# Rebuilding the low bits of three weight tiles on ScalarE instead of shifting on VectorE, in a retention and SwiGLU kernel

## The chip, the cores and the metric

The kernel runs on one core of a Trainium2 chip. The metric is the device time of one execution, in microseconds (us). Before the change it is 654.19 us, the median of three runs (653.77 to 654.31). Engines are called by the names of the profile: PE is TensorE's matmul, PEld its weight load, DVE is VectorE, ACT is ScalarE, POOL is GpSimd, SP is SyncE. SP issues most DMA transfers and computes nothing.

## What is computed

The reference is a retention layer (a linear attention with a decay for each head) whose output goes through an RMS norm and a SwiGLU block. Cut to what matters here:

```python
# attention: 4 x 8 heads x 768 x 64, blocks of 64, decay lam per head
out[:, :, sl] = intra + inter            # (q k^T * decay) v  +  (q * decay) state
x   = out as rows of tokens              # 3072 tokens x 512
rms = sqrt(mean(x * x, axis=-1) + 1e-06)
xn  = x / rms * rms_g
g   = xn @ w_gate                        # 512 x 1536
val = xn @ w_val                         # 512 x 1536
y   = (g * sigmoid(g) * val) @ w_out     # 1536 x 512
```

The three weight matrices arrive as float64, so each weight is 8 bytes in device memory. The kernel loads them as pairs of 32-bit words and builds a float32 from each pair itself, by shifts and an OR on the integer words. That conversion is what the change touches.

## The kernel before

**Tiles.** The 1536 hidden columns are 12 tiles `f` of 128, and the 3072 tokens are 6 groups `m` of 512. A unit `(m, f)` makes gate and val of one tile for one group, the SiLU and the product, and adds into the output. PE works with split operands: each weight and each activation is a high and a low half in fp16, and three products (high by high, low by high, high by low) stand for one.

**Start of the kernel.** Until about 37 us the kernel loads the first group's q, k and v, runs its retention on PE, forms the norm, and converts the first weight tiles. PE's first projection (`pg`, line 761) needs the normed activations `xn` (DVE, line 714), cast to a high half by ACT (`x`, line 719) and to a low half by DVE (line 722), and the split weights `wg`, `wv` of tile 0. From there on PE runs units of projection and output product (lines 780 to 782), with the retention of group 1 in between.

**The conversion of a tile** takes these steps, for gate and val together (128 x 1024 words) or, for tile 1, in two halves of 128 x 512:

- `lift` (line 218, ACT): reads the high word of each pair as a float, with a scale and a slope for negative numbers that put sign and exponent where the shift wants them, and writes `bits`.
- `convert` part 0 (line 227, DVE): `bits << 3`, in place.
- `convert` part 1 (line 230, DVE): `(low word >> 29) | bits`, which puts in the low three bits of the mantissa.
- `square` (line 440, ACT; rows named `junk`, followed by a read of the accumulator), then `norm` (line 445, PE; `pn`), `scale` (lines 452 and 456, DVE; `e` and `sc`), then `high` (line 463, ACT) and `low` (line 467, DVE), which split the tile into `wg` and `wv`.

The output weights of a tile (`raw_o`) go through `lift_o` and `convert_o`, which use the same two functions on 128 x 512, then a split into `wo` by ACT (line 246) and DVE (line 250).

**Buffers.** The raw pairs of tile 0 land in the tile `partial`, those of the later tiles in the four buffers `in` (named `raw_gv`), those of the output weights in the two buffers `raw_o`. The next load into a buffer is issued by SP, in order, once the step that reads it last is done (lines 87, 99 and 105 are the loads of q, k and v, of gate and val, and of the output weights). The PSUM bank `pg` holds the gate product of a unit, then the state sums `pst` (line 540) of the retention, so these wait for the SiLU `sg` (line 1022, ACT) that reads the gate product. The SBUF tiles of `sg` rotate with the squares `sq` (line 606), which POOL adds up (line 612).

**The order.** Each engine runs its instructions in the order in which they are written. A planner in the kernel (`Plan`) sets it before anything is built: each step has an engine, a cost and a due time, written out by hand in calls of `step(...)`, and a table of shifts moves single due times. The conversion of a tile is planned by `convert_steps` (`halved_steps` for tile 1), with ACT for the lift, 0.7 us of DVE for part 0 and 1.23 us for part 1.

Of the kernel before, what the change touches and what calls it, by code (L numbers as in the profile page):

```python
# [9 lines left out]
F32 = mybir.dt.float32  # L10
# [3 lines left out]
AF = mybir.ActivationFunctionType  # L14
ALU = mybir.AluOpType
PSUM = bass.MemoryType.PSUM

P = 128
G = 512
# [4 lines left out]
def retention_swiglu_kernel(  # L24
# [19 lines left out]
    nc = tc.nc  # L44
# [10 lines left out]
    const = ctx.enter_context(tc.tile_pool(name="const", bufs=1))  # L55
# [158 lines left out]
    def lift(bits, raw):  # L214

        nc.scalar.activation(
            bits.bitcast(F32), raw[:, :, 1].bitcast(F32), AF.Prelu, scale=2.0**-112,
            alpha=2.0**32,  # L220
        )

    def convert(bits, raw, part=None):


        if part != 1:
            nc.vector.tensor_single_scalar(bits, bits, 3, op=ALU.logical_shift_left)
        if part == 0:
            return
        nc.vector.scalar_tensor_tensor(  # L230
            bits, raw[:, :, 0], 29, bits, ALU.logical_shift_right, ALU.bitwise_or
        )
# [159 lines left out]
    class Weights:  # L392
# [22 lines left out]
        def lift(self, i=None):  # L415
            if not i:
                self.start()
            if i is None:
                lift(self.w, self.raw)
            else:  # L420
                lift(self.wi[i], self.raw[:, i * G : (i + 1) * G])

        def convert(self, i=None, part=None):
            if i is None:
                convert(self.w, self.raw, part)
            else:
                convert(self.wi[i], self.raw[:, i * G : (i + 1) * G], part)

        def lift_o(self):
            self.raw_o = raws.pop((self.f, "o"))  # L430
            lift(self.bits, self.raw_o)

        def convert_o(self, part=None):
            convert(self.bits, self.raw_o, part)
# [1452 lines left out]
```

## Time and profile before

| | |
|---|---|
| median of three runs | 654.19 us (653.77 to 654.31) |
| the profiled execution | 654.11 us, span 652.3 us |
| granted TensorE clock | 0.999 |
| busy, share of the span | PE 98%, DVE 67%, ACT 51%, POOL 23% |
| 27 to 37 us, of 10.00 | PE 8.46, DVE 9.52, ACT 9.08, POOL 3.48 |
| 40.5 to 47 us, of 6.50 | PE 6.44, DVE 6.20, ACT 5.19, POOL 1.28 |

The span runs from the first to the last instruction, and the execution's own time has 1.8 us more around it. In a row of the timeline the first number is the start in us from the span's start, the second the duration in us, then engine, line, operation, output `<-` input, shape and count; in brackets stands how long the engine sat idle before it and what ended the wait. Instructions of one engine overlap a little in such rows: the next one starts some 0.1 us before the last has ended.

### The profile page before, as it was taken

How to read it: one execution, taken by the hardware profiler on the slowest of the kernel's cores; microseconds unless marked ns; L12 is line 12 of the kernel's file. 1: busy time of each engine (PE TensorE's matmuls, PEld its weight loads, DVE VectorE, ACT ScalarE, POOL GpSimd, SP SyncE). 2: the span in 40 equal slices, each digit the busy share in tenths (PEclk: the TensorE clock that was granted, in tenths of full speed). 3: DMA queues.
4: the chain of work that ended last, by engine and by line, in shares of the span. 5: the costliest groups of instructions: out<-in, count | busy, mean ns of one | idle time of the engine just before them, and what ended most of it. 6: DMA issues, size and time to landing. Idle time of an engine off the chain costs nothing.

```text
span 652.3 us, 12342 instructions
## 1 busy us (share of the span) xinstructions
PE 642.5 (98%) x5016; PEld 442.0 (68%) x5016; DVE 433.9 (67%) x836; ACT 334.8 (51%) x676; POOL 149.4 (23%) x133
## 2 busy tenths in 40 slices
PE   7999999999999999999999999999999999999997
PEld 6846564755656645777777777777777777777774
DVE  6798897968997659656589634587543488544334
ACT  2876876756774444444545533335444334533332
POOL 2213040003477654354703011002010101100000
PEclk9999999999999999999999999999999999999999
DMA  8956653411002400101300311100220000000001
GB/s 328 327 211 221 238 191 133 169 58 65 1 24 91 146 2 1 65 4 63 130 2 2 130 65 65 66 1 1 97 99 1 2 2 1 33 33 1 2 1 65
DMA packets 14314, 51.13 MB, mean 78 GB/s; under 512 B 1713, under 2 KB 1969, under 8 KB 12849
## 3 DMA queue, kind: packets, MB, share of 16 engines
q1 hardware_dynamic: 13968, 50.21, 21.5%
q8 instruction: 39, 0.64, 0.4%
q10 hardware_dynamic: 288, 0.14, 0.1%
q14 instruction: 19, 0.15, 0.1%
HBM read 44.05 MB, written 6.29 MB: 77 GB/s over the span
## 4 chain that ended last, share of the span: by engine, by line
PE 95%; DVE 3%; DMA 1%; issue 0%; POOL 0%; ACT 0%; DVEq 0%; ACTq 0%
PE pa L948 20%; PE pb L948 15%; PE acc L780 10%; PE acc L782 10%; PE acc L781 10%; PE pg L761 9%; PE pv L761 9%; PE pa L507 4%; PE po L572 3%; PE po L583 3%; PE pst L540 2%; PE pss L628 1%; DMA cs<-in_consts_dram 1%; DVE xn L714 0%; DVE pw L159 0%
## 5 line engine op out<-in xcount | busy, mean ns | idle before, releaser
L996 ACT COPY tx<-pa 128x256 f32<-128x256 f32 x144 | 53.6, 372 | 136.6 <-PE pa L948 134.9
L782 PE MATMUL acc<-wo,hh 128*128 128x512 f16 (+1 forms) x288 | 110.2, 383 | 0.0
L781 PE MATMUL acc<-wo,hh 128*128 128x512 f16 (+1 forms) x288 | 110.1, 382 | 0.0
L1000 DVE TENSOR_TENSOR tx<-pb,tx 128x256 f32<-128x256 f32 x96 | 40.8, 425 | 65.3 <-PE pb L948 59.9
L780 PE MATMUL acc<-wo,hh 128*128 128x512 f16 x216 | 81.8, 379 | 0.0
L1004 DVE TENSOR_TENSOR sg<-pb,tx 128x256 f32<-128x256 f32 x48 | 20.4, 425 | 78.5 <-ACT tx L996 76.1
L948 PEld LDWEIGHTS <-wo 128*128 128x128 f16 x576 | 54.9, 98 | 23.2 <-issue 1.7
L761 PE MATMUL pg<-x,wg 128*128 128x512 f16 x288 | 67.7, 379 | 1.3 <-DVE wg L467 0.7
L761 PE MATMUL pv<-x,wv 128*128 128x512 f16 x288 | 67.5, 379 | 0.0
L948 PEld LDWEIGHTS <-wg 128*128 128x128 f16 x576 | 56.3, 98 | 16.2 <-issue 0.3
L1041 ACT CAST hh<-sg 128x512 f16<-128x512 f32 (+2 forms) x73 | 44.7, 612 | 35.6 <-DVE sg L1016 15.4
L948 PEld LDWEIGHTS <-wv 128*128 128x128 f16 x576 | 56.3, 98 | 8.3 <-issue 0.2
L531 POOL TENSOR_TENSOR qkv<-qkv,pw 128x512 f32<-128x512 f32 x24 | 32.2, 1342 | 77.3 <-PE pa L507 71.1
L761 PEld LDWEIGHTS <-wg 128*128 128x128 f16 x288 | 26.8, 98 | 33.8 <-issue 2.4
L761 PEld LDWEIGHTS <-wv 128*128 128x128 f16 x288 | 27.1, 98 | 32.9 <-issue 1.2
L1052 DVE TENSOR_TENSOR hh<-sg,hh 128x512 f16<-128x512 f32 x53 | 39.2, 739 | 7.8 <-ACT hh L1041 3.5
L1016 DVE SCALAR_TENSOR_TENSOR sg<-tx,cv,sg 128x512 f32<-128x512 f32 (+1 forms) x49 | 39.3, 803 | 5.6 <-ACT sg L1008 0.7
L948 PE MATMUL pa<-tx,wo 128*128 128x256 f16 x288 | 39.4, 273 | 0.0
L948 PE MATMUL pb<-tx,wo 128*128 128x256 f16 x288 | 39.3, 273 | 0.0
L948 PE MATMUL pa<-x,wv 128*128 128x256 f16 x288 | 39.3, 273 | 0.0
L948 PE MATMUL pa<-x,wg 128*128 128x256 f16 x288 | 39.3, 273 | 0.0
L948 PE MATMUL pb<-x,wv 128*128 128x256 f16 x288 | 39.3, 273 | 0.0
(186 smaller groups left out, 1152.1 us busy)
## 6 DMA issues: line engine op xcount, KB each, us to landing
qkv<-in_qkv_dram SPq DMA_DIRECT2D x48, 512.0 KB, 4.8
raw_gv<-in_weights_dram SPq DMA_DIRECT2D x11, 1024.0 KB, 6.3
raw_o<-in_weights_dram SPq DMA_DIRECT2D x12, 512.0 KB, 4.1
out_dram<-o SPq DMA_DIRECT2D x23, 256.0 KB, 2.1
partial<-in_weights_dram SPq DMA_DIRECT2D x2, 512.0 KB, 11.1
out_dram<-o ACTq DMA_DIRECT2D x1, 128.0 KB, 2.4
out_dram<-o SPq DMA_DIRECT2D x1, 128.0 KB, 2.4
cs<-in_consts_dram ACTq DMA_DIRECT2D x1, 8.0 KB, 4.7
```

What stands on the lines that cost most here:

```text
L507: nc.tensor.matmul(self.pa[j][:, c, :], self.kT[r, c, :], self.qT[r, c, :], start=True, stop=True,)
L531: eng.tensor_mul(self.qT, self.qT, pw[:, p : p + 1, :].broadcast_to([P, GC, P]))
L761: nc.tensor.matmul(ps, w[:, kk, :], x[:, kk, :], start=i == kk == 0, stop=i == 2 and kk == NK - 1,)
L780: nc.tensor.matmul(acc[:, cols], hl[:, ts_], oh, start=first, stop=False, skip_group_check=True)
L781: nc.tensor.matmul(acc[:, cols], hh[:, ts_], ol, start=False, stop=False, skip_group_check=True)
L782: nc.tensor.matmul(acc[:, cols], hh[:, ts_], oh, start=False, stop=last, skip_group_check=True)
L948: nc.tensor.matmul(ps, w(ow, k), x(ox, k), start=first and i == k == 0, stop=i == 2 and k == 1, skip_group_check=True,)
L996: nc.scalar.copy(self.kept[:, i], self.pa)
L1000: nc.vector.tensor_add(self.val[:, half], self.pb, self.kept[:, i])
L1016: nc.vector.scalar_tensor_tensor(sg, self.val[:, half], cv[:, self.f : self.f + 1], sg, ALU.mult, ALU.mult)
L1041: nc.scalar.copy(self.hh[:, half], self.sg[:, half])
L1052: nc.vector.tensor_sub(self.hl, self.sg, hh)
```

## The change

For tiles 0, 1 and 2 the low three bits are prepared by ACT. Behind the lift, ACT reads byte 3 of the low word (its top byte, `top`), computes `top / 32 - 15.5 / 32`, and the rounding to an integer on output gives `top >> 5`, which is `low word >> 29`. It is written over the low word in the raw buffer. DVE then needs one instruction instead of two: `(bits << 3) | low`. Part 0 of the DVE step issues nothing for these tiles. The constant `-15.5 / 32` is set once by POOL. Tiles 3 to 11 and all output weights are converted as before, and the planner's steps, costs and due times are the same.

```diff
+    shift = const.tile([P, 1], F32, name="shift")
+    nc.gpsimd.memset(shift, -15.5 / 32)
+
+    def low_bits(raw):
+        top = raw[:, :, 0].bitcast(mybir.dt.uint8)[:, :, 3]
+        nc.scalar.activation(raw[:, :, 0], top, AF.Identity, scale=1 / 32, bias=shift)
+
+    def join(bits, raw, part=None):
+        if part != 0:
+            nc.vector.scalar_tensor_tensor(
+                bits, bits, 3, raw[:, :, 0], ALU.logical_shift_left, ALU.bitwise_or
+            )
...
         def lift(self, i=None):
             if not i:
                 self.start()
             if i is None:
-                lift(self.w, self.raw)
+                w, raw = self.w, self.raw
             else:
-                lift(self.wi[i], self.raw[:, i * G : (i + 1) * G])
+                w, raw = self.wi[i], self.raw[:, i * G : (i + 1) * G]
+            lift(w, raw)
+            if self.f < 3:
+                low_bits(raw)
 
         def convert(self, i=None, part=None):
+            turn = join if self.f < 3 else convert
             if i is None:
-                convert(self.w, self.raw, part)
+                turn(self.w, self.raw, part)
             else:
-                convert(self.wi[i], self.raw[:, i * G : (i + 1) * G], part)
+                turn(self.wi[i], self.raw[:, i * G : (i + 1) * G], part)
```

The instructions stand as follows. ACT at tile 1, before: the squares of the first group's last head pair, the two lifts of tile 1, the lift of tile 0's output weights (`raw_o`), the split of tile 0, the second group's output and squares, and the squares of tile 1.

```order
L606 ACTIVATE sq_3_406<-po_3_343 128x512
L218 ACTIVATE w_0_424<-raw_gv_370 128x512
L218 ACTIVATE w_1_425<-raw_gv_370 128x512
L218 ACTIVATE wg<-raw_o_393 128x512
L463 ACTIVATE wg<-w_334,sc_441 128x512
L463 ACTIVATE wv<-w_334,sc_441 128x512
L595 COPY x_469<-po_0_432 128x512
L606 ACTIVATE sq_476<-po_0_432 128x512
L440 ACTIVATE junk_0_479,ssq_478<-w_0_424 128x512
```

ACT at tile 1, now (line numbers behind the new functions are larger by 18 or 22):

```order
L628 ACTIVATE sq_3_408<-po_3_346 128x512
L218 ACTIVATE w_0_426<-raw_gv_372 128x512
L231 ACTIVATE raw_gv_372<-raw_gv_372,shift 128x512
L218 ACTIVATE w_1_427<-raw_gv_372 128x512
L231 ACTIVATE raw_gv_372<-raw_gv_372,shift 128x512
L218 ACTIVATE wg<-raw_o_395 128x512
L485 ACTIVATE wg<-w_336,sc_445 128x512
L485 ACTIVATE wv<-w_336,sc_445 128x512
L617 COPY x_472<-po_0_436 128x512
L628 ACTIVATE sq_478<-po_0_436 128x512
L462 ACTIVATE junk_0_481,ssq_480<-w_0_426 128x512
```

Each lift has a second activation behind it, and all that follows keeps its order. ACT at tile 2, before: the SiLU of unit 0, the split of tile 1's val half, the lift of tile 2, the high half `hh` of unit 0's product, the split `wo` of tile 0's output weights, the SiLU of unit 1, and the squares of tile 2.

```order
L1022 ACTIVATE sg_0_554<-pg_0_510,cg 128x512
L463 ACTIVATE wv<-w_1_425,sc_523 128x512
L218 ACTIVATE w_563<-raw_gv_415 128x1024
L1041 CAST hh_0_578<-sg_0_554 128x512
L246 CAST wo_581<-wg 128x512
L1022 ACTIVATE sg_1_597<-pg_1_565,cg 128x512
L440 ACTIVATE junk_0_615,ssq_614<-w_563 128x512
```

ACT at tile 2, now:

```order
L1044 ACTIVATE sg_0_556<-pg_0_512,cg 128x512
L485 ACTIVATE wv<-w_1_427,sc_525 128x512
L218 ACTIVATE w_565<-raw_gv_417 128x1024
L231 ACTIVATE raw_gv_417<-raw_gv_417,shift 128x1024
L1063 CAST hh_0_581<-sg_0_556 128x512
L264 CAST wo_583<-wg 128x512
L1044 ACTIVATE sg_1_599<-pg_1_568,cg 128x512
L462 ACTIVATE junk_0_617,ssq_616<-w_565 128x512
```

The new activation stands ahead of the casts `hh` and `wo` and of unit 1's SiLU. DVE at tile 2, before: unit 0's product, the low half of tile 1's val, the shift of tile 2, the low half of tile 0's output weights, the OR of tile 2, and the decayed scores `a` of group 1.

```order
L1029 SCALAR_TENSOR_TENSOR sg_0_554<-pv_0_517,cg,sg_0_554 128x512
L467 SCALAR_TENSOR_TENSOR wv<-w_1_425,sc_523,wv 128x512
L227 TENSOR_SCALAR w_563<-w_563 128x1024
L250 TENSOR_TENSOR wo_581<-wg,wo_581 128x512
L230 SCALAR_TENSOR_TENSOR w_563<-raw_gv_415,w_563 128x1024
L527 TENSOR_TENSOR a_1_612<-pa_1_0_591,mask 128x512
```

DVE at tile 2, now:

```order
L1051 SCALAR_TENSOR_TENSOR sg_0_556<-pv_0_519,cg,sg_0_556 128x512
L489 SCALAR_TENSOR_TENSOR wv<-w_1_427,sc_525,wv 128x512
L268 TENSOR_TENSOR wo_583<-wg,wo_583 128x512
L237 SCALAR_TENSOR_TENSOR w_565<-w_565,raw_gv_417 128x1024
L549 TENSOR_TENSOR a_1_614<-pa_1_0_593,mask 128x512
```

The shift is gone, and the low half of the output weights, which reads ACT's cast `wo`, still stands ahead of the join.

## The prediction, made before the changed kernel ran

> **What bounds the kernel now.** I read the page first, then PE's waits by releaser, then the chain of waits up to 70 us, then the timeline of the three conversions that change.
>
> ```profile
> span 652.3 us, 12342 instructions
> PE 642.5 (98%) x5016; PEld 442.0 (68%) x5016; DVE 433.9 (67%) x836; ACT 334.8 (51%) x676; POOL 149.4 (23%) x133
> ```
>
> PE is busy in all but 9.8 us of the span, so a change on ACT and DVE is worth only what it does to PE's gaps. PE's waits between 14 and 75 us (us in total, times, longest):
>
> ```profile
> PE pg L761 <- DVE wg L467: 0.7, 1, 0.7
> PE pg L761 <- ACT x L719: 0.6, 2, 0.3
> PE pn L445 <- ACT junk L440: 0.5, 1, 0.5
> ```
>
> All three lie between 31 and 37.3 us, where PE waits for the first normed activations and the first split weights. The timeline there, around tile 1:
>
> ```profile
> 27.09 1.27 ACT L218 ACTIVATE w<-raw_gv 128x512 f32<-128x512 f32 x2
> 29.28 0.72 ACT L463 ACTIVATE wg<-w,sc 128x512 f16<-128x512 f32 x1 [0.35 <-DVE sc L456]
> 29.61 0.42 DVE L227 TENSOR_SCALAR w<-w 128x512 int32<-128x512 int32 x1
> 30.51 1.16 PE L661 MATMUL pr<-ident,y 128*128 128x128 f32 x8
> 30.67 0.42 DVE L227 TENSOR_SCALAR w<-w 128x512 int32<-128x512 int32 x1
> 31.12 0.69 DVE L230 SCALAR_TENSOR_TENSOR w<-raw_gv,w 128x512 int32<-128x512 int32 x1
> 31.73 2.71 DVE L714 SCALAR_TENSOR_TENSOR xn<-x,gs,pr 128x512 f32<-128x512 f32 x4
> 32.51 2.65 ACT L719 CAST x<-xn 128x512 f16<-128x512 f32 x4 [0.18 <-DVE xn L714]
> 34.37 1.89 DVE L722 TENSOR_TENSOR x<-xn,x 128x512 f16<-128x512 f32 x3
> 35.20 0.38 PE L761 MATMUL pg<-x,wg 128*128 128x512 f16 x1 [0.34 <-ACT x L719]
> 37.23 1.90 PE L761 MATMUL pg<-x,wg 128*128 128x512 f16 x8 [0.67 <-DVE wg L467]
> ```
>
> Two things are to be seen. DVE goes without a break from the second join of tile 1 into `xn` at 31.73. And `xn` multiplies by `pr`, whose matmuls end at 30.51 + 1.16 = 31.67: the two arrive within 0.1 us of each other. From 37.23 us PE has hardly a gap to the end. So the most that could be won lies ahead of 37.23, and whatever makes PE stand still later is lost for good.
>
> **Tile 0** comes first, and its change is nearly free.
>
> ```profile
> 19.62 1.17 ACT L218 ACTIVATE w<-partial 128x1024 f32<-128x1024 f32 x1
> 21.93 1.23 DVE L230 SCALAR_TENSOR_TENSOR w<-partial,w 128x1024 int32<-128x1024 int32 x1
> L218 ACT ACTIVATE w<-raw_gv 128x1024 f32<-128x1024 f32 x9 | 10.2, 1136 | 0.0
> L218 ACT ACTIVATE w<-raw_gv 128x512 f32<-128x512 f32 x2 | 1.3, 694 | 0.0
> L595 ACT COPY x<-po 128x512 f32<-128x512 f32 x8 | 4.7, 585 | 5.2 <-PE po L583 5.1
> ```
>
> No row shows ScalarE reading single bytes or writing words at a stride. The nearest row is the lift: it reads the same pairs at the same 8-byte step, in the same shapes, in 1.136 us (wide) and 0.694 us (narrow). I take that for the new activation. From below it is bounded by the plain copy, 0.585 us for 512 columns; on the lift's slope (1.136 - 0.694 = 0.442 for 512 more) that is 1.03 us wide. From above I allow twice the lift, 2.27 and 1.39 us, in case bytes or strided writes go at half speed. Behind another instruction each adds some 0.1 us less than its duration, since ACT's rows overlap by that much: the two narrow lifts start 1.27 - 0.694 = 0.58 us apart. The new DVE join has the shapes and types of the one it replaces, so it costs the same 1.23 or 0.69 us.
>
> The lift at 19.62 and the new activation end at 19.62 + 1.07 + 1.14 = 21.83; the join before started at 21.93, behind the shift. It can now start at the same time or 0.1 us earlier, and nothing on PE hangs on that moment (no wait of PE is listed between 14 and 31 us). Zero.
>
> The Trainium skill has a price for it in "ScalarE: Activation LUTs" (What ACT_TABLE_LOAD costs): about 280 ns and 0.833 ns for each column when the bias is a pointer, which makes 1.13 and 0.71 us; the sum by these would be the same.
>
> **Tile 1.** DVE loses two shifts of 0.42 us. ACT gains two narrow activations, each worth 0.58 us, so 1.16 us. The split at 29.28 had 0.35 us of idling before it, 0.45 with the overlap, so it comes 1.16 - 0.45 = 0.7 us late. Ahead of the casts of `x` ACT waits another 0.18 us, 0.28 with the overlap, so the first cast starts about 0.4 us late, at 32.9. From there ACT gains: the four casts are paced by `xn` (2.71 us for four, some 0.68 apart) and can follow each other every 0.52 (the casts at 41.75 and 42.27, shown below, do), so the fourth starts at 34.5, as before. PE's matmul at 35.20, which waits for that cast, does not move. The first two matmuls of `pg` come later, behind the unread matmuls that PE runs while it waits, but PE waits again at 35.20 and 37.23 anyway.
>
> On DVE the second join ends 0.8 us earlier, at about 31.0. But `xn` cannot start before `pr` has ended, at 31.67, and stays at 31.7. `pr` does not move either: PE comes to it straight from the matmuls before. So the whole 0.84 us saved turns into DVE's wait for `pr`, and the gain is 0.05 us or less. Tile 1 is worth zero, from -0.05 to 0.
>
> **Tile 2.** Here PE is already at work, and the order of ACT matters.
>
> ```profile
> 40.60 1.13 ACT L218 ACTIVATE w<-raw_gv 128x1024 f32<-128x1024 f32 x1
> 41.75 0.62 ACT L1041 CAST hh<-sg 128x512 fp32r<-128x512 f32 x1
> 42.27 0.61 ACT L246 CAST wo<-wg 128x512 fp32r<-128x512 f32 x1
> 42.29 0.69 DVE L227 TENSOR_SCALAR w<-w 128x1024 int32<-128x1024 int32 x1
> 42.92 0.69 DVE L250 TENSOR_TENSOR wo<-wg,wo 128x512 fp32r<-128x512 f32 x1
> 43.53 1.22 DVE L230 SCALAR_TENSOR_TENSOR w<-raw_gv,w 128x1024 int32<-128x1024 int32 x1
> 43.85 0.69 ACT L1022 ACTIVATE sg<-pg,cg 128x512 f32<-128x512 f32 x1 [0.97 <-PE pg L761]
> 44.84 0.63 ACT L440 ACTIVATE junk<-w 128x512 bf16<-128x512 f32 x1 [0.30 <-DVE w L230]
> 46.13 0.19 ACT L440 ACTIVATION_READ_ACCUMULATOR junk<-w 128x1 f32 x1
> 46.83 0.17 PE L445 MATMUL pn<-ssq,ones_b 128*128 128x2 bf16 x1
> ```
>
> The shift at 42.29 was not what the join waited for. DVE's queue has `wo` low (42.92) ahead of the join, and that waits for ACT's cast `wo`, which ended at 42.27 + 0.61 = 42.88. ACT now runs lift, low bits, `hh`, `wo`: with the lift at 40.60 and 1.04 us for each wide one, `hh` starts at 42.65 instead of 41.75, `wo` at 43.17 instead of 42.27, and ends at 43.78. So `wo` low starts at 43.82, 0.9 us late, and DVE, free from 42.29 where the shift began, idles until then: 0.69 us of work is removed and 1.5 us of waiting put in. The join moves from 43.53 to 44.43, the squares from 44.84 to 45.74, the last read of their accumulator from 46.13 to 47.03, ending at 47.22. PE reached `pn` at 46.83 with those sums ready at 46.32. Now it comes there at 46.83 and waits until about 47.27: **+0.43 us** on PE, which nothing later gives back. Queued behind `wo` low on DVE are also the decayed scores of group 1 and the join of the output weights.
>
> The SiLU of unit 1 is hidden: it stood idle 0.97 us, ending at 43.85, and with `wo` starting 0.9 us later ACT is free at 43.7. If that cover were gone, PE's `pst` behind it would wait too, but the stall at `pn` would swallow it.
>
> **What the late DVE then does to a load.**
>
> ```profile
> 46.51 0.69 DVE L230 SCALAR_TENSOR_TENSOR wg<-raw_o,wg 128x512 int32<-128x512 int32 x1
> 47.23 0.33 SPq L105 DMA_DIRECT2D raw_o<-in_weights_dram  x1
> 51.60 0.67 ACT L218 ACTIVATE wg<-raw_o 128x512 f32<-128x512 f32 x1 [0.50 <-DMA raw_o<-in_weights_dram]
> 53.33 2.04 POOL L612 TENSOR_TENSOR sq<-sq,sq 128x512 f32<-128x512 f32 x1 [2.78 <-ACT sq L606]
> 55.40 0.69 ACT L1022 ACTIVATE sg<-pg,cg 128x512 f32<-128x512 f32 x1 [1.36 <-POOL sq L612]
> 56.14 0.57 PE L540 MATMUL pst<-qkv 128*64 128x64 f32 x12
> ```
>
> The output weights' join at 46.51 stands behind all this on DVE and moves by the same 0.9 us. It frees the buffer of the load issued at 47.23, and ACT's lift at 51.60 already waits for that load. It lands 0.9 us late if it takes as long as before. Behind the lift, ACT copies and squares, POOL adds at 53.33, unit 2's SiLU at 55.40 waits for POOL's buffer, and PE's `pst` starts 0.05 us after that SiLU ends (55.40 + 0.69 = 56.09). This whole row moves with the load, and PE is then 0.9 us late instead of 0.43: another **+0.47 us**. If the loads ahead of it in flight leave it more room and it lands as much as 0.47 us sooner after its issue, the addition is zero. After 56.14 DVE, ACT and PE are late by the same amount, so no further wait grows.
>
> **The sum.** 0 (tile 0) + 0 (tile 1) + 0.43 + 0.47 = 0.9 us at most, 0.43 at least, with the lift's durations. The activation's lower bound (0.1 us less) takes off 0.1. I take 0.8, nearer the upper end, because the row at 51.60 shows ACT already waiting for the load. The profiled execution took 654.11 us (span 652.3 and 1.8 around it), 0.08 us under the median of 654.19; on the median the forecast is 655.0 us. That is 0.12% slower. A measurement of this kernel can tell about 0.2%, 1.3 us, from no change.
>
> A rule of the Trainium skill speaks against the change: "ScalarE: Activation LUTs" (Rules for kernel authors) wants additions and products on VectorE, which is faster for each element. The trace agrees, 0.693 us for the wide shift by this row against 1.136 for the lift:
>
> ```profile
> L227 DVE TENSOR_SCALAR w<-w 128x1024 int32<-128x1024 int32 x10 | 6.9, 693 | 1.3 <-ACT w L218 1.3
> ```
>
> By the rule alone, with nothing overlapped, the change would cost 2 x (1.136 - 0.693) + 2 x (0.694 - 0.42) = 1.4 us.
>
> **Rivals.** *The activation is slow* (slower). If bytes at a stride, or the strided write, cost twice the lift, tile 2 alone takes 1.13 us more than in the sum. At tile 1 the two narrow ones take 1.4 us more; the fourth cast may be late by 0.4 us unseen, since the last of the three `x` lows (34.37, 1.89 us in all) starts only at about 35.6 while the casts ended at 32.51 + 2.65 = 35.16, and the other 1.0 falls on PE. Total 0.8 + 1.13 + 1.0 = 2.9: 657.1 us. It decides (over 1.3 us) from a wide activation of about 1.55 us. Against it stands the lift, which reads at the same step without any loss against its own contiguous write; nothing in the trace speaks on the write. Chance 0.23.
>
> *VectorE is the bound* (faster). DVE is busy 9.52 of the 10 us from 27 to 37:
>
> ```profile
> 27.00:37.00 10.00, 8.46 (x83) 6.09 (x79) 9.52 (x22) 9.08 (x18) 3.48 (x3) 1.00 0.75 259
> ```
>
> If its queue alone set 37.23, and the removed shifts counted in full, the time would fall by 0.84 us at tile 1 and 0.69 at tile 2, to 652.7 us. "Perfetto Trace Analysis" of the Trainium skill (Optimizing Scalar/DVE Operations) says as much: with VectorE saturated, moving work to ScalarE may make sense. The 31.67 end of `pr` and ACT's own 9.08 us in the same row speak against it. Chance 0.05.
>
> *All of it is hidden*: the load lands in time and the sums are ready sooner than the rows say. 654.2 to 654.5 us, no change. Chance 0.12.
>
> **How the numbers follow.** The forecast, +0.4 to +1.2 us, has 0.60. It and the hidden case are within 0.2%: 0.72. Slower by more: the slow activation, 0.23. Faster by more: 0.05. The forecast's own range is 654.5 to 655.4. For 8 in 10 the range goes down to the hidden case, 654.1, with the spread of the runs, and half way into the slow activation, 656.6.
>
> **What would show it.** Right: new rows on ACT of about 1.1 and 0.7 us; DVE waiting for `pr` ahead of `xn` with `xn` still at 31.7; PE at 37.2 as before; DVE idle over 1 us ahead of `wo` low at 43.8; PE waiting 0.4 us at tile 2's `pn`; ACT's wait for `raw_o` ending near 52.5 and `pst` near 57.0. Wrong: `xn` well before 31.6 (then `pr` is not what holds it), the matmuls at 37.23 moved, wide activations over 1.5 us, or a PE stall at some step after 57 us.

## The result, and the profile after

The changed kernel takes 659.00 us (median of five runs, 656.46 to 659.96) where the kernel before takes 654.19 us (653.77 to 655.41). On the medians the change costs 4.8 us. The ratio is 1.0058, with a 95% interval from 1.004 to 1.0076, which is 3.8 us (2.6 to 5.0). The forecast was 0.8. The profiled execution took 659.38 us, 5.27 us more than the one of before. Of the five runs, two had TensorE at full clock throughout and took 656.46 and 657.03; three, the profiled one among them, show a mean granted clock of 0.997.

The page of the changed kernel, first part (busy time, share, instructions):

```profile
span 657.6 us, 12342 instructions
PE 644.9 (98%) x5016; PEld 443.0 (67%) x5016; DVE 431.2 (66%) x832; ACT 337.5 (51%) x680; POOL 149.6 (23%) x134
```

DVE has lost 2.7 us of work, ACT has gained 2.7, and PE is busy 2.4 us longer with the same number of instructions. PE's waits between 14 and 75 us (us in total, times, longest) say where the rest is:

```profile
PE pv L783 <- ACT sq L628: 3.0, 1, 3.0
PE pn L467 <- ACT junk L462: 1.6, 2, 1.2
PE pg L783 <- DVE wg L489: 0.7, 1, 0.7
PE pn L467 <- DVE e L474: 0.2, 1, 0.2
```

The third stood there before. Of the second, 1.2 us and the 0.2 us of the fourth lie ahead of 37 us. PE waited there before too, 1.8 us in all; now it is 2.1. New, after 37 us, are 0.4 us at `pn` and 3.0 us at `pv`.

The timeline of the changed kernel at tiles 0 and 1:

```profile
20.36 1.24 ACT L231 ACTIVATE partial<-partial,shift 128x1024 int32<-128x1024 uint8 x1
27.35 0.78 ACT L231 ACTIVATE raw_gv<-raw_gv,shift 128x512 int32<-128x512 uint8 x1
30.19 1.16 PE L683 MATMUL pr<-ident,y 128*128 128x128 f32 x8
31.38 2.72 DVE L736 SCALAR_TENSOR_TENSOR xn<-x,gs,pr 128x512 f32<-128x512 f32 x4 [0.81 <-PE pr L683]
37.19 1.90 PE L783 MATMUL pg<-x,wg 128*128 128x512 f16 x8 [0.67 <-DVE wg L489]
```

DVE's saved 0.84 us at tile 1 has become 0.81 us of waiting for `pr`, and the matmuls that stood at 37.23 stand at 37.19. But this execution was already 0.32 us ahead at tile 0's lift (19.30 for 19.62), before any new instruction. From the start of `pr` to these matmuls it took 7.00 us, and before 6.72. The 0.3 us arise at the low halves of `x`, of which POOL makes one and DVE three. In the kernel before, POOL's row was this, and DVE's stood at 34.37, 1.89 us long:

```profile
33.20 1.16 POOL L722 TENSOR_TENSOR x<-xn,x 128x512 f16<-128x512 f32 x1 [3.14 <-ACT x L719]
```

and now:

```profile
33.31 1.17 POOL L744 TENSOR_TENSOR x<-xn,x 128x512 f16<-128x512 f32 x1 [3.58 <-ACT x L741]
34.02 2.20 DVE L744 TENSOR_TENSOR x<-xn,x 128x512 f16<-128x512 f32 x3
```

Counted from `pr`, POOL starts 0.43 us later, since the first cast of `x` is that late behind the new activations. Before, POOL had ended (34.36) when DVE began. Now it runs beside DVE's first low half for 0.46 us, and DVE's row is 0.31 us longer. The seven traces that have the change at tile 1 take 6.99 to 7.04 us from `pr` to these matmuls, the five without it 6.71 to 6.72. That POOL's work beside it is what slows DVE is likely, but no run here tests it.

The timeline at tile 2:

```profile
41.62 1.22 ACT L231 ACTIVATE raw_gv<-raw_gv,shift 128x1024 int32<-128x1024 uint8 x1
43.25 0.61 ACT L264 CAST wo<-wg 128x512 fp32r<-128x512 f32 x1
43.89 0.69 DVE L268 TENSOR_TENSOR wo<-wg,wo 128x512 fp32r<-128x512 f32 x1 [1.56 <-ACT wo L264]
44.50 1.22 DVE L237 SCALAR_TENSOR_TENSOR w<-w,raw_gv 128x1024 int32<-128x1024 int32 x1
45.79 0.33 SPq L99 DMA_DIRECT2D raw_gv<-in_weights_dram  x1
47.34 0.16 PE L467 MATMUL pn<-ssq,ones_b 128*128 128x2 bf16 x1 [0.44 <-ACT junk L462]
48.20 0.33 SPq L105 DMA_DIRECT2D raw_o<-in_weights_dram  x1
```

This is the chain of the forecast, to 0.1 us: cast, wait of DVE, join, `pn`. But two loads are issued late, not one: the row at 45.79 is a load of gate and val into the buffer that tile 2's join has just read. Then comes what was not forecast:

```profile
55.32 0.67 ACT L218 ACTIVATE wg<-raw_o 128x512 f32<-128x512 f32 x1 [3.71 <-DMA raw_o<-in_weights_dram]
55.89 0.57 ACT L617 COPY x<-po 128x512 f32<-128x512 f32 x1
56.36 0.60 ACT L628 ACTIVATE sq<-po 128x512 f32<-128x512 f32 x1
57.01 4.42 PE L783 MATMUL pv<-x,wv 128*128 128x512 f16 x12 [3.01 <-ACT sq L628]
```

ACT waits 3.71 us for the load. Behind that lift stand, in ACT's order, the copy and the squares of `po`, which read the PSUM bank that PE's next `pv` writes; so PE waits 3.01 us. In the kernel before the same rows were these:

```profile
44.82 0.33 SPq L99 DMA_DIRECT2D raw_gv<-in_weights_dram  x1
52.64 0.61 ACT L606 ACTIVATE sq<-po 128x512 f32<-128x512 f32 x1
53.34 2.75 PE L761 MATMUL pv<-x,wv 128*128 128x512 f16 x12
```

There the squares end at 52.64 + 0.61 = 53.25, 0.09 us before the `pv` that needs the bank. The same twelve matmuls also take 4.42 us now instead of 2.75. The stretches of the changed kernel around them (us, their length, busy time of PE, PEld, DVE, ACT, POOL, then the granted clock) show why:

```profile
57.00:58.00 1.00, 0.99 (x5) 0.48 (x5) 0.00 (x0) 0.75 (x2) 0.96 (x1) 0.96 1.01 406
58.00:59.00 1.00, 1.00 (x4) 0.30 (x2) 0.00 (x0) 0.66 (x2) 0.31 (x1) 0.50 0.93 385
60.00:61.00 1.00, 1.00 (x4) 0.26 (x2) 0.00 (x0) 1.00 (x4) 0.00 (x0) 0.50 0.00 0
61.00:62.00 1.00, 1.00 (x16) 0.56 (x16) 0.01 (x1) 0.19 (x1) 0.00 (x0) 0.83 0.00 0
```

The granted clock falls to half at about 57.9, 0.9 us after the matmuls have begun again (the first stretch still has 0.96), and stays there for about 3.4 us. That is 1.7 of the 2.4 us by which PE is busy longer. So the profiled 5.27 us are 0.44 (`pn`) + 3.01 (`pv`) + 1.67 (4.42 - 2.75) = 5.12, with the 0.3 us of tile 1 and the 0.32 us of the earlier start nearly cancelling, and less than 0.2 us that no wait names. After that PE loses nothing more.

The load itself is what has grown. Issues between 44 and 50.5 us (KB each, us from issue to landing), before:

```profile
raw_gv<-in_weights_dram SPq DMA_DIRECT2D x1, 1024.0 KB, 5.5
raw_o<-in_weights_dram SPq DMA_DIRECT2D x1, 512.0 KB, 4.4
```

and after:

```profile
raw_gv<-in_weights_dram SPq DMA_DIRECT2D x1, 1024.0 KB, 7.6
raw_o<-in_weights_dram SPq DMA_DIRECT2D x1, 512.0 KB, 7.1
```

Issued 0.97 us later, the load of the output weights lands 3.71 us later.

### The profile page after: what moved, and what is told of

It is laid out like the page before. It is cut to its first block, busy times and chain, and to the rows that moved or that the text cites. A ratio compares the mean times of both kernels' runs of the same rounds, so it can differ in the third digit from the quotient of the medians.

```text
span 657.6 us, 12342 instructions
## 1 busy us (share of the span) xinstructions
PE 644.9 (98%) x5016; PEld 443.0 (67%) x5016; DVE 431.2 (66%) x832; ACT 337.5 (51%) x680; POOL 149.6 (23%) x134
## 4 chain that ended last, share of the span: by engine, by line
PE 93%; DVE 3%; DMA 2%; ACT 1%; issue 0%; DVEq 0%
PE pa L970 19%; PE pb L970 14%; PE acc L802 10%; PE acc L804 9%; PE acc L803 9%; PE pv L783 9%; PE pg L783 8%; PE pa L529 4%; PE po L594 3%; PE po L605 3%; PE pst L562 2%; DMA raw_o<-in_weights_dram 1%; PE pss L650 1%; DMA cs<-in_consts_dram 1%; PE pr L683 0%; DVE xn L736 0%
## 5 line engine op out<-in xcount | busy, mean ns | idle before, releaser
L783 PE MATMUL pv<-x,wv 128*128 128x512 f16 x288 | 69.4, 386 | 3.0 <-ACT sq L628 3.0
```

The costliest lines, as they stand in the source:

```text
L783: nc.tensor.matmul(ps, w[:, kk, :], x[:, kk, :], start=i == kk == 0, stop=i == 2 and kk == NK - 1,)
```

## The experiments

Theory: the new activation, by its place on ACT ahead of `wo`, delays tile 2's join, with it two loads, and these take longer than before when issued late; ACT stands behind the second of them with the two instructions that free PE's bank. Rivals: the early tiles cost something (ACT is late through all of the ramp); the strided byte read and write disturb something of their own; the stall comes from DVE and ACT being late, and the load only goes with it. Ratios below are against the kernel before, timed beside each kernel on the same chip: its median was 654.4 us for the experiments on the tiles and the place, 655.19 for those on the late load, the order and the clock, and 654.38 for those on the path and the whole repair.

### Which tile

```diff
-            if self.f < 3:
+            if self.f < 2:
                 low_bits(raw)
...
-            turn = join if self.f < 3 else convert
+            turn = join if self.f < 2 else convert
```

The tiles 0 and 1 alone; in a second kernel the two conditions read `self.f == 2`, tile 2 alone.

> The change for tiles 0 and 1 alone; tile 2 is converted as before. Theory A (the loss comes from the place of tile 2's activation on ACT, ahead of the cast of the output weights): nothing is lost, 654.2 us, within 0.5 of the kernel before, no wait of PE at tile 2's pn, load of the output weights of tile 3 issued at 47.2 and landed at about 51.6. Rival B (writing the low word back into a raw buffer makes the later loads slow): part of the loss stays, over 655.5 us.

> The change for tile 2 alone; tiles 0 and 1 as before. Theory A: all of the loss, 656.5 to 660 us as with the whole change, PE waits 0.4 us at pn and 2 to 3 us at unit 2's val product, and the granted clock halves for some us where that wait is near 3 us. If tiles 0 and 1 carried part of it, it comes out 1 us or more under the whole change.

Tiles 0 and 1 alone: 654.3 us, ratio 0.9995 (0.998 to 1.0011), with no wait of PE between 38 and 75 us. The 0.3 us of tile 1 are in its trace (7.01 us from `pr` to `pg`), but they are 0.05%, too little for these runs to tell. Tile 2 alone: 658.52 us, 1.0052 (1.0034 to 1.0071). PE's long wait with tile 2 alone:

```profile
54.16 0.67 ACT L218 ACTIVATE wg<-raw_o 128x512 f32<-128x512 f32 x1 [2.91 <-DMA raw_o<-in_weights_dram]
55.85 2.75 PE L783 MATMUL pv<-x,wv 128*128 128x512 f16 x12 [2.22 <-ACT sq L628]
```

All of the loss that these runs can tell is tile 2's. After this wait of 2.22 us the matmuls kept their 2.75 us: in this execution the clock did not fall.

### The instruction, or its place

```diff
-            if self.f < 3:
+            if self.f < 2:
                 low_bits(raw)
...
+            if fn == hs[0].silu:
+                low_bits(raws[2].rearrange("p k w o -> p (k w) o"))
             fn(*args)
```

First, the change for all three tiles, with tile 2's low bits issued ahead of unit 0's SiLU, some 3.8 us earlier and no longer between the lift and `wo`.

> The whole change, but tile 2's activation stands earlier on ACT, ahead of unit 0's SiLU, where ACT sat idle 1.34 us for DVE. The same instructions, the same writes into the raw buffers. Theory A: 654.2 us within 0.5, the cast of the output weights back at 42.3, the load issued at 47.2. Rival B: the loss stays, over 656 us, since the raw buffer is written just the same.

Second, the kernel before with ACT's lift of tile 2 issued twice: the same output, and no byte or strided write.

```diff
                 lift(self.w, self.raw)
+                if self.f == 2:
+                    lift(self.w, self.raw)
```

> The kernel before, with tile 2's lift done twice (the same result, one more wide activation at the same place on ACT, no write into the raw buffer, VectorE's shift kept). Theory A: the same loss as the whole change, 656 to 660 us, with the cast of the output weights 1.0 us late and the load issued at about 48.2. Rival B: 654.2 to 655, nothing but the 0.4 us at pn.

The change with the early low bits takes 654.68 us, ratio 1.0008 (0.9987 to 1.003): most of the loss is gone with the same work on the same engine. Its profile still has a wait of 0.95 us at `pv`, which was not expected: the load of the output weights was issued in time (47.07) and yet took 5.4 us. The doubled lift takes 658.4 us, 1.0052 (1.0033 to 1.0071), as much as the change at tile 2, and PE waits at the same place:

```profile
PE pv L763 <- ACT sq L608: 2.3, 1, 2.3
PE pn L447 <- ACT junk L442: 0.4, 1, 0.4
```

So it is 1.1 us of any work at this place of ACT's queue. The rival of bytes and strided writes falls.

### The late load alone

The kernel before, in which a one-column subtraction on POOL, written just ahead of the load of gate and val, reads the buffer into which it goes. The load then leaves at 46.04 instead of 44.82; nothing on ACT or DVE has changed.

```diff
+            if fn is load_next and pending[0] == (load_gv, 4):
+                hold = const.tile([P, 1], F32, name="hold")
+                word = first_weights[2].raw[:, 0:1, 1].bitcast(F32)
+                nc.gpsimd.tensor_sub(hold, word, word)
```

> The kernel before, with a one-column subtraction on POOL that reads tile 2's raw words late, so that the load of tile 4's gate and val into that buffer is issued at about 46.1 instead of 44.8. Nothing on ACT or DVE changes. Theory A with a slow load (the load itself takes 7 us or more when it starts after the loads ahead have drained): output weights of tile 3 land after 53.5, 656 to 660 us. Rival (the load takes 5.5 us whenever it starts): they land by 52.9 and the loss is 1.3 us or less.

657.7 us, ratio 1.003 (1.0013 to 1.0048), within what was expected. Its timeline:

```profile
46.04 0.33 SPq L99 DMA_DIRECT2D raw_gv<-in_weights_dram  x1
47.10 0.33 SPq L105 DMA_DIRECT2D raw_o<-in_weights_dram  x1
53.49 0.67 ACT L218 ACTIVATE wg<-raw_o 128x512 f32<-128x512 f32 x1 [2.51 <-DMA raw_o<-in_weights_dram]
55.19 2.75 PE L761 MATMUL pv<-x,wv 128*128 128x512 f16 x12 [1.81 <-ACT sq L606]
```

The load of the output weights is issued as early as in the kernel before (47.10 against 47.23) and still lands 1.9 us later, since the load ahead of it is late. This rules out that ACT or DVE have to be late for the loss.

### The order of the two loads

```diff
         order = plan.run()
+        fns = [(plan.steps[i][3].__name__, *plan.steps[i][4]) for _, i in order]
+        o3 = fns.index(("load_o", 3))
+        gv4 = max(j for j in range(o3) if fns[j][0] == "load_next")
+        order.insert(o3, order.pop(gv4))
```

The load of the output weights goes ahead of that of gate and val in SP's order; in the changed kernel, and then in the kernel before.

> The changed kernel, with two loads exchanged in SP's order: tile 3's output weights ahead of tile 4's gate and val. Theory A (the big loss is this load standing in line behind tile 4's 1 MB): it is issued at about 48.2, lands in some 3.5 us, at 51.7, and PE loses only the 0.4 us at pn: 654.6 to 655.2 us. Rival (ACT's lateness itself costs the rest): still over 656 us.

> The kernel before, with the same two loads exchanged. Theory A: the load is issued at about 47.3, lands at 50.8, and PE's slack is as before: 653.7 us, and the runs at 655 to 658 us that the kernel before also shows become rare, if they come from this load. Rival: no difference, 654.4 with the same spread.

The changed kernel with the loads exchanged: 655.86 us, 1.0012 (0.9998 to 1.0025). By the ratios some 3 us of the loss are gone, but not all, and the time lies above the 654.6 to 655.2 that were expected: the load took 5.2 us and not 3.5, so ACT still waited 1.8 us and PE 1.1:

```profile
53.59 0.67 ACT L218 ACTIVATE wg<-raw_o 128x512 f32<-128x512 f32 x1 [1.84 <-DMA raw_o<-in_weights_dram]
55.29 2.75 PE L783 MATMUL pv<-x,wv 128*128 128x512 f16 x12 [1.15 <-ACT sq L628]
```

The kernel before with the loads exchanged: 653.72 us, 0.9981 (0.9968 to 0.9994), faster than both kernels. The load takes 3.9 us there and ACT does not wait for it. Where the 0.2% come from is not shown: neither this profile nor that of the kernel before has a wait at `pv`, and of the 0.58 us between these two executions 0.43 lie ahead of `pr`, where the kernels are alike. Its rows:

```profile
47.20 0.43 SPq L99 DMA_DIRECT2D raw_gv<-in_weights_dram  x1
50.00 1.44 ACT L218 ACTIVATE wg<-raw_o 128x512 f32<-128x512 f32 x2
52.90 2.75 PE L761 MATMUL pv<-x,wv 128*128 128x512 f16 x12
```

### The path from the load to PE

The changed kernel with its late load, but with ACT's lift of that load moved behind unit 2's SiLU, so that the copy and the squares no longer stand behind it.

```diff
         order = plan.run()
+        fns = [plan.steps[i][3] for _, i in order]
+        lift3 = fns.index(first_weights[3].lift_o)
+        silu2 = fns.index(hs[2].silu)
+        order.insert(silu2, order.pop(lift3))
```

> The changed kernel with all its instructions, but ScalarE's lift of the late load (raw_o) stands behind unit 2's SiLU and no longer ahead of the copy and the squares that free the bank of TensorE's pv. The load is issued as late as in the changed kernel. If the loss of 3 us and the fallen clock come through these two instructions, TensorE's wait at pv is gone, the wait of 0.4 us at pn stays, and the time is 0.4 to 0.7 us above the kernel before: 654.6 where the kernel before takes 654.2 (ratio 1.0005 to 1.0012). If the late load itself costs time in another way (transfers in each other's way, later loads late in turn), the loss stays at 3 us or more: 657 or above, with TensorE waiting elsewhere between 50 and 75 us.

654.62 us, ratio 1.0003 (0.9991 to 1.0014). Timeline and waits:

```profile
47.56 0.16 PE L467 MATMUL pn<-ssq,ones_b 128*128 128x2 bf16 x1 [0.45 <-ACT junk L462]
48.42 0.33 SPq L105 DMA_DIRECT2D raw_o<-in_weights_dram  x1
52.20 0.59 ACT L628 ACTIVATE sq<-po 128x512 f32<-128x512 f32 x1
54.06 2.75 PE L783 MATMUL pv<-x,wv 128*128 128x512 f16 x12
54.94 0.70 ACT L218 ACTIVATE wg<-raw_o 128x512 f32<-128x512 f32 x1
```

The load is as late as ever (issued at 48.42, landed 6.5 us later, at 54.91), `pn` still waits 0.45 us, and `pv` waits for nothing. What is left, 0.2 us on the medians and 0.6 in the profiles, is no more than the `pn` term and tile 1's 0.3 us. So the loss reaches PE only through the two instructions behind the lift. This is the plainest proof of the chain.

### The clock

The changed kernel with eight unread matmuls ahead of the `pv` that waits, so that PE works through most of the wait.

```diff
+            if fn == hs[2].val and args[0] == 0:
+                busy(8)
```

> The changed kernel, with eight unread matmuls (some 2 us) on PE ahead of unit 2's val product, where PE waited 3 us. Theory A (in the runs at 659 us 1.7 us of the loss is TensorE at half its granted clock after that wait): the wait left behind them is near 1 us, the clock stays at 1.0 and all runs lie between 656 and 658 us. Rival (the clock does not matter, the load alone makes 659): the spread stays, up to 660.

657.55 us, 1.0039 (1.0024 to 1.0055), by the ratios 1.2 us less of a loss than in the changed kernel, with intervals that overlap. The runs reach from 656.52 to 660.03, and five of twelve lie above the 658 up to which they were expected. In its profile the clock stays at 1.00 where it fell before, and the matmuls have their old length:

```profile
57.96 2.75 PE L783 MATMUL pv<-x,wv 128*128 128x512 f16 x12 [0.47 <-ACT sq L628]
9.00:12.00 3.00, 2.32 (x16) 1.97 (x16) 2.32 (x7) 0.91 (x2) 0.00 (x0) 0.72 1.00 365
12.00:15.00 3.00, 3.00 (x33) 2.53 (x34) 2.48 (x10) 0.21 (x1) 1.27 (x1) 0.71 1.03 421
```

The last two rows, stretches of the same kernel, show that this execution had its half clock elsewhere, between 9 and 15 us. That costs it up to 1.7 us (0.28 and 0.29 of 3 us each). In this execution, then, the shorter wait left the clock alone. The gain in time fits the clock's 1.67 us, but the spread does not let it be read to better than 1 us.

### All of it repaired

The changed kernel with the early low bits and the exchanged loads: the two edits shown above, together.

> All three tiles with ScalarE's low bits, those of tile 2 ahead of unit 0's SiLU, and the load of the output weights ahead of the load of gate and val in SyncE's order. If position and load are all there is to the loss, no wait of TensorE is left between 40 and 75 us, and the time is that of the kernel before with the loads swapped: 653.7 (653.5 to 654.2), ratio 0.997 to 0.999. If ScalarE's extra 5 us of work or the write into the raw buffer cost something of their own that the waits did not show, it stays 0.5 us or more above that: 654.3 or more, ratio 0.9995 or above.

654.23 us, ratio 0.9997 (0.9986 to 1.0008). No wait of PE is left between 38 and 75 us, as expected. But the time lies 0.5 us above the 653.72 of the kernel before with the loads exchanged, and the ratio is not the expected 0.997 to 0.999: it lies where it was to lie if the change still cost something of its own (0.9995 or more). That work is some 4 us by the rows, not the 5 written there. The two kernels were timed on different chips, and the interval reaches to both readings. The traces speak for a cost: from `pr` to `pg` it is 7.01 us here and 6.71 there, the 0.3 us of tile 1. The change brings no gain in any case: the kernel before with the two loads exchanged has the lowest median.

## Why the prediction was wrong

**Tile 0** was right, and tile 1 up to `xn`. The activation takes 1.24 and 1.22 us wide, 0.78 and 0.77 us narrow, where the lift's 1.136 and 0.694 were assumed; the bounds held, and the alternatives of a slow activation (from 1.55 us) and of VectorE as the bound fell. The estimate from the Trainium skill's price in "ScalarE: Activation LUTs" (What ACT_TABLE_LOAD costs), 1.13 and 0.71 us, is as far off as the lift's row. DVE waited for `pr` as forecast, and tiles 0 and 1 alone measured 0.9995. But "Tile 1 is worth zero" is off by 0.3 us. The text had the first cast of `x` 0.4 us late, as measured (0.43), and followed only the fourth. It left out POOL's low half of `x`, which reads the first cast and was pushed into DVE's row. It was luck that the profiled matmuls still stood at 37.19: that execution had started 0.32 us early. PE's two short waits for the casts of `x` were drawn together into one of 1.21 us at `pn`.

**Tile 2 up to `pn`** was right: `wo` low at 43.89 for 43.82, DVE's idle time 1.56 for 1.5, the stall 0.44 for 0.43, the SiLU hidden, the issue of the load at 48.20 for 48.13.

**The step that failed** is "It lands 0.9 us late if it takes as long as before", with its term of +0.47 us. The load took 7.10 us instead of 4.36, ACT was 3.7 us late, and the term measured 3.01. Three things went wrong in it:

- The range of the step had only one side. It allowed that the load lands sooner after its issue, never later, though the loads ahead of it were named. The load directly ahead, gate and val, is issued behind the very join that the step before had just moved by 0.97 us. It was not priced at all, and in the kernel with the late load alone it makes about half of the loss by itself (0.30% of 0.58%).
- The place was wrong. The text led the late load through POOL's sum to `pst`, where 1.36 us of ACT's waiting lay between. PE meets it earlier, at `pv`, through the copy and the squares, where the kernel before had 0.09 us to spare. The rows were there to read: PE's `pv` at 53.34 right behind squares that end at 53.25.
- The clock was no term of the sum. A stall that grows to 3 us was followed by 3.4 us of half clock, which made 1.67 us of 5.27.

With the measured sizes the sum is 0 (tile 0) + 0.30 (tile 1) + 0.44 + 3.01 + 1.67 = 5.4 us, and with the 0.32 us of the earlier start taken off, 5.1 of the 5.27. The direction of each step behind tile 1 stood; the size of one, and a consequence of that size, did not. The chance given to more than 0.2% slower went to a slow activation, and no alternative had the load in it.

**What stays open** is why a load issued later takes longer. Landing times of the trace, with "ahead" as the time from the issue of the gate and val load to the landing of the load before it:

| kernel | issued ahead | landed behind the load before | output weights, behind that |
|---|---|---|---|
| before | 3.0 us | 2.5 us | 1.2 us |
| tiles 0 and 1 alone | 2.8 | 2.5 | 1.3 |
| early low bits | 2.8 | 3.7 | 1.3 |
| changed | 2.0 | 5.6 | 1.9 |
| changed, lift of the load late | 2.0 | 4.5 | 2.4 |
| tile 2 alone | 1.9 | 5.2 | 1.6 |
| changed, eight unread matmuls | 1.9 | 5.6 | 1.2 |
| lift twice | 1.8 | 5.7 | 1.2 |
| before, late load | 1.4 | 4.8 | 1.2 |

A 1 MB load in 2.5 us is 420 GB/s. With 2.8 us or more in hand a load can follow the one before at that rate; with some 2 us or less it never did, and took 2 to 3 us more. The early low bits had 2.8 us in hand and took 1.2 us more all the same, so the time of issue is not all of it. The rates of the whole core go with the table: from 46 to 50 us they were 440 and 401 GB/s in each 2 us before, and 244 and 311 after. What the engines do in that time, no run here separates.

## What to carry to other kernels

When a step moves, list every load that waits for its buffer and every instruction queued behind the one that reads the load, and give a load's duration a far end above as well as below: the same load took 4.4 us in one of these kernels and 7.1 in another. Work moved off a busy engine costs by its place in the other engine's queue, not by its duration; here 1.2 us on an engine that is 51% busy cost 4.8 us, and the same 1.2 us placed 3.8 us earlier 0.3 us on the medians (0.5 by the ratio, with an interval from -0.9 to 2.0). Follow every reader of an instruction that comes late, also on the engines that the sum leaves out: a cast that came 0.43 us late, and that POOL reads, went with 0.3 us here. Where an engine comes to a buffer only 0.1 us after it is freed, look at what stands ahead of the instruction that frees it: exchanging two loads ahead of that place gained 0.2% by itself, though not by a wait that a profile here shows, while the change, at its best, gained nothing.

## What the runs showed of the hardware

- After PE's wait of 3.01 us the granted clock was 0.50 for 3.4 us, from 0.9 us behind the wait on; after waits of 2.22 and 2.25 us (tile 2 alone, lift twice) the next twelve matmuls kept their 2.75 us. The Trainium skill says in "TensorE: Matmul & The Clock Gate" (What's actually happening) that the clock halves after an idle window of about 3.4 us that runs freely. The length of the slow stretch agrees; the wait here was shorter than a whole window.
- The activation from single bytes to 32-bit words at an 8-byte step costs 0.07 to 0.1 us more than the lift with the same shape, so neither the bytes nor the strided write run at a lower rate: the difference between the wide and the narrow one, 0.44 to 0.47 us for 512 columns, is the lift's 0.44.
- DVE's three low halves of `x` took 1.89 us where POOL's had ended before them, and 2.20 us where POOL's ran beside the first of them for 0.46 us. No run here separates the cause.
- A load's time from issue to landing was 3.8 to 7.1 us for the same 512 KB, and 5.3 to 7.6 us for the same 1024 KB, with other times of issue and other loads ahead of it. What sets the time is open.
